# Attention inputs laid out by the host, softmax of phi along rows, and a new list for the first 48 half-blocks

## The chip, the core and the metric

The program runs on one core of a Trainium2 chip. A core has TensorE (PE in the profile; its weight loads are PEld), VectorE (DVE), ScalarE (ACT) and GpSimd (POOL), which work side by side, each on its own instructions in order, and SyncE (SP), which here issues nearly all transfers (DMAs). The metric is the device time of one execution in microseconds (us); lower is better.

## What is computed

```python
# q, k, v: (8, 8, 576, 64), phi: (8, 8, 576, 32); heads 8, tokens 576
a = exp(phi - max(phi, axis=2));  a = a / (sum(a, axis=2) + 1e-09)       # softmax over the 576 tokens
k_m = einsum('bhsm,bhsd->bhmd', a, k);  v_m = einsum('bhsm,bhsd->bhmd', a, v)
scores = q @ k_m.transpose / sqrt(64);  attn = softmax(scores, axis=-1)  # over 32 memory slots
x = (attn @ v_m), heads side by side: (4608, 512)
h = x @ moe_w_in;   x = (h - tanh(h)) @ moe_w_out                        # 512 -> 2048 -> 512
h = x @ moe2_w_in;  y = elu(h) @ moe2_w_out
```

The weights come as 64-bit floats, the rest as 32-bit ones.

## The kernel before

**Attention** runs in 16 units, one for each batch element and half of its heads (four heads, `unit`, line 260). A unit loads phi, k with v, and q with 96 partitions of six tokens each (`load`, line 241). It takes the maximum of phi over the six tokens of a partition on VectorE (`cmax`, line 278), transposes that (`mT`, 290), reduces it again (`nmax`), spreads it over partitions by a diagonal matrix and a product with ones (`dmax`, `bmax`, 299, copied to `bm`, 305), subtracts it and takes the exponential (`a`, 309 and 314). `km` (321) are 24 products (six token groups by four heads) of 192 columns: 64 of k, 64 of v and 64 of ones, whose product is the softmax's sum. The scaled result `kvs` is transposed (`kT_ps`, 357) into `kT` and `vm`. q is transposed by twelve `pq` (348), each three copied by ScalarE to `qT` (350). `sc` (375) are the scores; VectorE transposes them, softmax follows (382 to 389), and the weights of attention, split in a high and a low part, go as `p` to memory (`p_dram`) and come back by `load_p`; those of the first batch element stay on the chip.

**The first layer** (`Moe1`) folds `vm` into the input weight (`vw_unit`, `vw_ps`) and runs in 128 half-blocks: of 16 blocks of 288 tokens by 4 quarters of the hidden width, two halves each. A half-block is twelve `h_ps` products of 288 columns (`h_unit`, 500), an activation in steps on ScalarE, VectorE and GpSimd (`g_a` to `g_lo`), and, some half-blocks later, groups of twelve `x_ps` products (`x_unit`, 568), two groups per half-block in the mean. **Weights** are read as raw 64-bit words (`raw`, 741 and 744), turned into 32-bit floats by `convert` (188 to 206) and split in high and low; conversions c0 to c15 serve the first half-blocks, c16 to c53 make the second layer's weights and write them to `w_dram`. **The second layer** (`Moe2`) follows and takes the second half of the time; its output rows are stored in pieces, since the token order of the units is not that of the output.

**What sets the order** is a list written as numbers. `BEGIN` is run through first and then `SCRIPT`, one line for each half-block. A single letter is a step of that half-block (H its `h_ps`, A, a, s, B, R, d, e, p, G, g its activation, X or Y one `x_ps` group with its copy on ScalarE or VectorE, V and W the folding of `vm`), `u5` advances attention unit 5 to its next `yield`, `c7` conversion 7. Each engine's instructions, and SP's transfers, stand in the order in which the list calls them, and wait there for what they need. `POOLS` says for each unit which steps GpSimd takes from VectorE, `WHERE` the same for each conversion. `BESIDE` and two further places put products of the identity (`keep_busy`, 212) into PE's order, whose result nobody reads.

Of the kernel before, what the change touches and what calls it, by code (L numbers as in the profile page):

```python
# [213 lines left out]

class Attention:

# [43 lines left out]
    def unit(self, u, nxt, where, first_p=None):  # L260
# [33 lines left out]
        if spaced:  # L294
            yield
# [797 lines left out]
```

## Time and profile before

| | us |
|---|---|
| median of 3 runs | 1622.95 (1622.79 to 1624.86) |
| the profiled execution, its own time | 1623.58 |
| its span, first to last instruction | 1621.8 |
| PE busy in the span | 1574.3 |
| VectorE, ScalarE, GpSimd busy | 1135.9, 906.6, 748.2 |

The rows below are of that execution. A busy time says that an engine has an instruction under way; groups of matmuls overlap their neighbours, so the busy times of the groups of one engine may add to more than the engine's own. "idle before" is the time that the engine stood still in front of an instruction, with the engine or transfer that ended it.

### The profile page before, as it was taken

The page shows a single profiled execution, that of the slowest core. Times are in us where ns is not written, and L with a number is a line of the kernel's source. Part 1 is how long each engine was busy: PE and PEld are TensorE (multiplying, and loading weights), DVE is VectorE, ACT ScalarE, POOL GpSimd, SP SyncE. Part 2 cuts the span into 40 slices and gives each one's busy share as a digit, 9 for nine tenths or more (in the row PEclk, how much of TensorE's full clock was granted, in tenths as well). Part 3 has the DMA queues.
Part 4 walks back from the last instruction along what each step waited for, and adds up shares of the span by engine and source line. Part 5 has one row for each costly group of instructions (what it writes and reads, how often), then busy time and mean ns, then how long its engine had stood idle before and what let it go on. Part 6 is the DMA issues. An engine that isn't in the chain of part 4 may idle for free.

```text
span 1621.8 us, 28087 instructions
## 1 busy us (share of the span) xinstructions
PE 1574.3 (97%) x10762; PEld 1374.9 (85%) x10762; DVE 1135.9 (70%) x1642; ACT 906.6 (56%) x1641; POOL 748.2 (46%) x534
## 2 busy tenths in 40 slices
PE   5799999999999999999999999999999999999998
PEld 3578889888999999999999888888888888888886
DVE  4988688989888888887655655565565655555644
ACT  2657788888878888888733333333333333333332
POOL 1446667777756677776623322322322223222222
PEclk9779999999999999999999999999999999999999
DMA  9776697796645676674793212112121212121100
GB/s 224 212 207 202 197 264 232 200 287 229 218 139 174 205 220 221 220 221 160 250 370 128 73 40 78 53 50 81 40 91 40 78 40 78 39 65 52 39 1 26
DMA packets 142214, 232.91 MB, mean 144 GB/s; under 512 B 8704, under 2 KB 102912, under 8 KB 140032
## 3 DMA queue, kind: packets, MB, share of 16 engines
q1 hardware_dynamic: 141648, 230.39, 46.0%
q8 instruction: 85, 1.39, 0.4%
q10 hardware_dynamic: 432, 0.72, 0.1%
q14 instruction: 49, 0.40, 0.1%
HBM read 157.68 MB, written 73.40 MB: 142 GB/s over the span
## 4 chain that ended last, share of the span: by engine, by line
PE 86%; DVE 4%; DMA 3%; POOL 2%; ACT 2%; issue 2%; SPq 0%; ACTq 0%; POOLq 0%; DVEq 0%
PE h_ps L628 25%; PE o_ps L675 24%; PE x_ps L568 21%; PE h_ps L500 11%; PE vw_ps L482 2%; DMA raw<-in_moe_w_in_dram 1%; PE km L321 1%; DVE s L538 1%; DMA kv<-in_k_dram 1%; POOL v L524 1%; POOL g L553 1%; DMA x_dram<-x 1%; PE pq L348 0%; PE sc L375 0%; DVE s L542 0%
## 5 line engine op out<-in xcount | busy, mean ns | idle before, releaser
L654 POOL TENSOR_TENSOR e<-hm,e 128x512 fp32r<-128x512 f32 x144 | 186.8, 1297 | 573.5 <-ACT e L653 530.5
L568 PE MATMUL x_ps<-g,w 128*128 128x288 f32 x3072 | 437.4, 297 | 4.4 <-DVE vw L487 2.5
L568 PEld LDWEIGHTS x_ps<-g,w 128*128 128x128 f32 x3072 | 415.9, 189 | 13.0 <-DVE vw L487 5.0
L628 PE MATMUL h_ps<-x,wi 128*128 128x512 f32 (+1 forms) x1920 | 422.1, 370 | 0.0
L675 PE MATMUL o_ps<-wo,e 128*128 128x512 f32 x1728 | 420.2, 392 | 0.0
L628 PEld LDWEIGHTS h_ps<-x,wi 128*128 128x128 f32 x1920 | 336.0, 188 | 65.7
L675 PEld LDWEIGHTS o_ps<-wo,e 128*128 128x128 f32 x1728 | 323.7, 188 | 71.5 <-POOL e L654 0.4
L639 ACT ACTIVATE t_ps<-hm 128x512 f32<-128x512 f32 x144 | 86.7, 602 | 499.2 <-DVE hm L638 499.2
L553 POOL TENSOR_TENSOR g<-s,g 128x576 fp32r<-128x576 f32 x128 | 199.2, 1556 | 105.8 <-ACT g L548 84.7
L645 DVE SCALAR_TENSOR_TENSOR hm<-hm,t_ps 128x512 f32<-128x512 f32 x144 | 98.9, 687 | 200.3 <-ACT hm L640 200.3
L500 PE MATMUL h_ps<-p,vw 128*128 128x288 f32 x1536 | 234.3, 302 | 0.1
L524 POOL TENSOR_TENSOR v<-t,u 128x576 f32<-128x576 f32 x128 | 185.7, 1451 | 96.2 <-ACT u L515 77.6
L500 PEld LDWEIGHTS h_ps<-p,vw 128*128 128x128 f32 x1536 | 213.1, 191 | 13.9 <-issue 13.2
L638 DVE TENSOR_SCALAR hm<-h_ps 128x512 f32<-128x512 f32 x144 | 99.5, 691 | 126.7 <-PE h_ps L628 124.0
L538 DVE SCALAR_TENSOR_TENSOR s<-s,v 128x576 f32<-128x576 f32 x128 | 135.8, 1061 | 39.6 <-ACT big L528 27.9
L511 ACT ACTIVATE t<-h_ps 128x576 f32<-128x576 f32 x128 | 83.4, 652 | 74.3 <-issue 30.6
L542 DVE COPY_PREDICATED s<-big,h_ps 128x576 f32<-128x576 uint32 x128 | 106.4, 832 | 9.6 <-ACT big L528 1.3
L519 ACT ACTIVATE s<-u,bias 128x576 f32<-128x576 f32 x128 | 99.5, 777 | 12.1 <-POOL g L553 4.6
L533 DVE TENSOR_TENSOR h_ps<-h_ps,t 128x576 f32<-128x576 f32 x128 | 96.9, 757 | 10.4 <-ACT u L515 10.4
L646 DVE SCALAR_TENSOR_TENSOR hm<-hm,t_ps 128x512 f32<-128x512 f32 x144 | 98.9, 687 | 5.0
L647 DVE TENSOR_TENSOR hm<-hm,h_ps 128x512 f32<-128x512 f32 x144 | 98.9, 687 | 5.0
L528 ACT ACTIVATE big<-u,bias 128x576 f32<-128x576 f32 x128 | 98.2, 767 | 4.9 <-DVE s L542 4.6
(100 smaller groups left out, 1536.1 us busy)
## 6 DMA issues: line engine op xcount, KB each, us to landing
x_dram<-x SPq DMA_DIRECT2D x128, 288.0 KB, 3.2
xr<-x_dram SPq DMA_DIRECT2D x72, 512.0 KB, 3.7
p<-p_dram SPq DMA_DIRECT2D x62, 576.0 KB, 5.4
raw<-in_moe_w_in_dram SPq DMA_DIRECT2D x32, 512.0 KB, 4.3
raw<-in_moe_w_out_dram SPq DMA_DIRECT2D x32, 512.0 KB, 4.4
w_dram<-wst SPq DMA_DIRECT2D x32, 512.0 KB, 4.5
kv<-in_k_dram SPq DMA_DIRECT2D x16, 576.0 KB, 6.7
kv<-in_v_dram SPq DMA_DIRECT2D x16, 576.0 KB, 8.5
```

The costliest lines, as they stand in the source:

```text
L500: nc.tensor.matmul(ps[:, j, :NB], lhsT=vw[a][:, kc, c0 + 128 * j:c0 + 128 * j + 128], rhs=p[:, kc, b, :], start=(k == 0), stop=(k == 5))
L519: self.nc.scalar.activation(s, u, ACTF.Square, bias=self.const["bias"][:, 0:1], scale=G_S)
L524: nc.gpsimd.tensor_tensor(v, t, u, op=ALU.mult)
L538: nc.vector.scalar_tensor_tensor(s, s, G_B, v, op0=ALU.add, op1=ALU.mult)
L542: self.nc.vector.copy_predicated(s, big.bitcast(U32), d)
L553: self.nc.gpsimd.tensor_tensor(g[:, 1], s, r32(g[:, 0]), op=ALU.subtract)
L568: nc.tensor.matmul(ps, lhsT=wo[pg][a][:, j, 128 * dm:128 * dm + 128], rhs=self.g[n, pg][:, b, j, :], start=(k == 0), stop=(k == 11))
L628: nc.tensor.matmul(out, lhsT=w3[:, a, kc, 128 * j:128 * j + 128], rhs=x[:, b, kc, :], start=(i == 0), stop=(i == 11))
L638: nc.vector.tensor_scalar(hm, w[0], 0.0, None, op0=ALU.min)
L645: nc.vector.scalar_tensor_tensor(hm, hm, 1.0, t, op0=ALU.add, op1=ALU.mult)
L654: nc.gpsimd.tensor_tensor(e[:, 1], hm, r32(e[:, 0]), op=ALU.subtract)
L675: nc.tensor.matmul(acc, lhsT=e[:, a, jj, 128 * tg:128 * tg + 128], rhs=w4[:, b, j, :], start=(k == 0 and jj == 0 and (a, b) == (0, 0)), st ...
```

## The change

**Layout.** Numpy now lays the inputs out before the launch. phi is 128 rows (four heads by 32 slots) of 576 tokens, so one row holds all tokens of a slot. q is stored transposed as `sc` reads it. k and v are stored together, 128 tokens in a row group, 18 groups of which the last two hold the remaining 64 tokens of two heads each. Weights are stored as pages of 128 rows of 4 KB, as `raw` reads them. A unit has three loads in place of five.

**The unit.** The maximum is one reduction along the row; the exponential takes it as bias and also gives the sum. Four transposes `aT` and two small products `tail` bring the exponentials to tokens on partitions; ScalarE (for the larger part in two units VectorE) copies them to `a`. `km` are 16 products of 128 columns and four over 64 rows. `mT`, `dmax`, `bmax`, `bm`, the subtraction, `pq` and `qT` are gone, and with the token order the split stores of the output. The loads of k and v come one step earlier, that of q after `sc`; one pause (`yield`) of later units goes.

**The rest.** `BEGIN` and the first 48 of the 128 lines of `SCRIPT` are new, the other 80 are as before. `POOLS` and `WHERE` are new, and `BESIDE` is empty. `convert` may take the copy of the high part to GpSimd, the pools of `raw` and `cv` have five and three buffers for three and two. Letters for further engine choices (Q, T, O, N, E) are added; the list uses none of them.

```diff
-POOLS = ("", "lm", "alm", "almd", "amlk", "al", "damls", "amk", "ld", "alds", "dams", "amltd", "daml", "daml", "dalk", "dalk")
-WHERE = "ggss...g.g...g............g...............................gss..."
-BESIDE = {("km", 2): 10, ("bmax", 3): 10, ("km", 3): 5, ("sc", 2): 5, ("sc", 3): 9, ("bmax", 5): 3}
+POOLS = ("sl", "mks", "lmsk", "msl", "sl", "sk", "", "e", "lk", "ls", "msk", "mlk", "m", "mlsek", "lk", "lk")
+WHERE = "..s.gb.g:ggb.g:.g.s..g:.g:g...............................gss..."
+BESIDE = {}
...
-    nc.scalar.activation(hi, a, ACTF.Copy)
+    if hi_pool:
+        nc.gpsimd.tensor_copy(hi, a)
+    else:
+        nc.scalar.activation(hi, a, ACTF.Copy)
...
-        self.kv = fix.tile([96, 3, 4, 6, D], F32, name="kv")
-        self.a = fix.tile([96, 6, 4, M], F32, name="a")
+        self.kv = fix.tile([128, 18, 2, D], F32, name="kv")
+        self.a = fix.tile([128, 18, M], F32, name="a")
...
-            t = self.phi_p.tile([96, 4, 6, M], F32, tag="phi", name="phi")
-            nc.sync.dma_start(out=t, in_=view("phi", 0, 4))
+            t = self.phi_p.tile([128, S], F32, tag="phi", name="phi")
         else:
-            t = self.q_p.tile([96, 2, 6, D], F32, tag="q", name="q")
-            nc.sync.dma_start(out=t, in_=view("q", 0 if what == "q0" else 2, 2))
+            t = self.q_p.tile([128, 4, NB], F32, tag="q", name="q")
+        self.nc.sync.dma_start(out=t, in_=self.ins[what][b, g])
...
-        nc.tensor.matmul(bmax, lhsT=self.ones[:, :96], rhs=dmax, start=True, stop=True)
...
+        nmax, rs = (sm.tile([128, 1], F32, tag=x, name=x) for x in ("nmax", "rs"))
+        nc.vector.tensor_reduce(nmax, e, axis=AX.X, op=ALU.max, negate=True)
+        yield
+        nc.scalar.activation(e, e, ACTF.Exp, bias=nmax, accum_out=rs)
+        yield
...
+        for c in range(4):
+            nc.tensor.transpose(aT[:, 128 * c:128 * c + 128], e[:, 128 * c:128 * c + 128], ident)
+        for r in (slice(0, 64), slice(64, 128)):
+            nc.tensor.matmul(tail[r, :64], lhsT=e[r, 512:], rhs=ident[r, r], start=True, stop=True)
+        if "e" in where:
+            nc.vector.tensor_copy(a[:, :16].rearrange("p c m -> p (c m)"), aT)
+        else:
+            nc.scalar.activation(a[:, :16].rearrange("p c m -> p (c m)"), aT, ACTF.Copy)
+        nc.scalar.activation(a[:, 16:].rearrange("p c m -> p (c m)"), tail[:, :64], ACTF.Copy)
...
-        for c in range(6):
+        for c in range(4):
             for h in range(4):
-                nc.tensor.matmul(kmv[32 * h:32 * h + 32], lhsT=a[:, c, h, :], rhs=kv[:, :, h, c, :],
-                                 start=(c == 0), stop=(c == 5))
+                nc.tensor.matmul(kmv[32 * h:32 * h + 32], lhsT=a[:, 4 * c + h], rhs=kv[:, 4 * c + h], start=(c == 0), stop=False)
+        for i in range(2):
+            for j in range(2):
+                h, r = 2 * j + i, slice(64 * j, 64 * j + 64)
+                nc.tensor.matmul(kmv[32 * h:32 * h + 32], lhsT=a[r, 16 + i], rhs=kv[r, 16 + i], start=False, stop=True)
...
-                    nc.tensor.transpose(pq[:, c2, :], qt[:, h, 2 * c2:2 * c2 + 2, :].rearrange("p c d -> p (c d)"),
-                                        ident[:96, :96])
-                nc.scalar.activation(qT[:, 2 * pr + h], pq, ACTF.Copy)
...
+        "phi": heads(inputs["phi"]).transpose(0, 1, 2, 4, 3).reshape(B, 2, 128, S),
+        "moe_w_in": w_in(inputs["moe_w_in"]), "moe_w_out": w_out(inputs["moe_w_out"]),
```

One line of the list shows the kind, that of the twelfth half-block (H11):

```diff
-          "X W H A a R V B s L u6 l d G u7 g e X p",
+          "X W G L H u5 A a u7 s u5 Y d V R u7 l g B e p u8 u8",
```

**Where instructions move.** The first place is PE from the scores of units 0 and 1 to the first half-block, before (`ident` as an input marks a transpose, or on line 212 a product that nobody reads; `x24` is a count):

```order
L375 MATMUL sc<-qT,kT 32x288 x16
L212 MATMUL km<-ident 128x128 x10
L321 MATMUL km<-kv,a 32x192 x24
L290 MATMUL mT<-ident,cmax 128x96
L482 MATMUL vw_ps<-w_317,vm 32x256 x8
L348 MATMUL pq<-ident,q 128x96 x6
L212 MATMUL bmax<-ident 128x128 x10
L299 MATMUL bmax<-dmax,ones 96x128
L357 MATMUL kT_ps<-ident,kvs 128x128 x2
L482 MATMUL vw_ps<-w_409,vm 32x256 x8
L212 MATMUL h_ps<-ident 128x128 x9
L500 MATMUL h_ps<-p,vw 128x288 x12
```

and now, where two units' scores directly follow their `kT_ps`:

```order
L317 MATMUL kT_ps<-ident,kvs 128x128 x4
L334 MATMUL sc<-q,kT 32x288 x16
L278 MATMUL aT<-ident,phi 128x128 x4
L280 MATMUL tail<-ident,phi 64x64 x2
L440 MATMUL vw_ps<-w_219,vm 32x256 x8
L294 MATMUL km<-kv,a 32x128 x16
L298 MATMUL km<-kv,a 32x128 x4
L278 MATMUL aT<-ident,phi 128x128 x4
L280 MATMUL tail<-ident,phi 64x64 x2
L440 MATMUL vw_ps<-w_293,vm 32x256 x8
L317 MATMUL kT_ps<-ident,kvs 128x128 x2
L214 MATMUL h_ps<-ident 128x128 x9
```

The transposes of q are gone from there, and in their place stand the `aT` and `tail` of units 2 and 3.

The second place is ScalarE around the exponentials of units 0 and 1 (`s_122` and `s_123` before, `s_120` and `s_121` now), before:

```order
L350 ACTIVATE qT<-pq 128x288 x4
L305 ACTIVATE bm<-bmax 96x128
L188 ACTIVATE cv_a<-raw 128x512 x2
L385 ACTIVATE s_122<-s_122 128x18x32
L385 ACTIVATE s_123<-s_123 128x18x32
L314 ACTIVATE a<-a 96x4x6x32
```

and now:

```order
L272 ACTIVATE phi,rs<-phi,nmax 128x576
L318 ACTIVATE kT<-kT_ps 128x128
L320 ACTIVATE vm<-kT_ps 64x128
L284 ACTIVATE a<-aT 128x512
L285 ACTIVATE a<-tail 128x64
L344 ACTIVATE s_120<-s_120 128x18x32
L344 ACTIVATE s_121<-s_121 128x18x32
```

Before, two conversions' first steps, each waiting for its `raw` page, stood directly ahead of the two exponentials; now the copies of unit 2 do.

The third place is the head of SP's transfers, before:

```order
L254 DMA phi<-in_phi_dram 96x4x192 x2
L250 DMA kv<-in_k_dram 96x4x384
L251 DMA kv<-in_v_dram 96x4x384
L250 DMA kv<-in_k_dram 96x4x384
L251 DMA kv<-in_v_dram 96x4x384
L257 DMA q<-in_q_dram 96x2x384 x3
L741 DMA raw<-in_moe_w_in_dram 128x2x256
L254 DMA phi<-in_phi_dram 96x4x192
L257 DMA q<-in_q_dram 96x2x384
L741 DMA raw<-in_moe_w_in_dram 128x2x256 x2
```

and now:

```order
L693 DMA raw<-in_moe_w_in_dram 128x512
L248 DMA phi<-in_phi_dram 128x576
L248 DMA q<-in_q_dram 128x1152
L248 DMA phi<-in_phi_dram 128x576
L693 DMA raw<-in_moe_w_in_dram 128x512
L248 DMA kv<-in_kv_dram 128x2304
L248 DMA phi<-in_phi_dram 128x576
L248 DMA kv<-in_kv_dram 128x2304
L693 DMA raw<-in_moe_w_in_dram 128x512
L248 DMA phi<-in_phi_dram 128x576
L248 DMA q<-in_q_dram 128x1152
L248 DMA kv<-in_kv_dram 128x2304
```

A unit's loads are three where they were five, and two weight pages stand among the first five transfers, where the first stood tenth.

## Rows read from the trace of the kernel before

**Rows 1.** Busy shares (part 1) and tenths in 40 slices of the span (part 2).

```profile
PE 1574.3 (97%) x10762; PEld 1374.9 (85%) x10762; DVE 1135.9 (70%) x1642; ACT 906.6 (56%) x1641; POOL 748.2 (46%) x534
...
DMA  9776697796645676674793212112121212121100
```

**Rows 2.** Table by stretch: us, then busy us (instructions) per engine, clock, DMA.

```profile
0.00:57.91 57.91, 35.26 (x314) 24.22 (x315) 36.14 (x69) 17.25 (x41) 11.54 (x19) 0.91 0.91 212
57.91:160.03 102.12, 89.72 (x847) 76.49 (x845) 88.92 (x130) 67.79 (x135) 59.60 (x44) 0.87 0.73 212
160.03:389.19 229.16, 223.88 (x2290) 202.01 (x2282) 195.12 (x299) 189.36 (x376) 160.51 (x114) 1.00 0.78 231
389.19:1621.80 1232.61, 1225.40 (x7326) 1072.16 (x7324) 815.75 (x1147) 632.18 (x1089) 516.54 (x358) 1.00 0.36 118
```

**Rows 3.** PE's timeline up to 165: start us, us, engine, line, operation [idle before].

```profile
12.36 4.07 PE L321 MATMUL km<-kv,a 96*32 96x192 f32 x48 [2.71 <-ACT a L314]
...
31.53 2.17 PE L375 MATMUL sc<-qT,kT 64*32 64x288 f32 x32
33.63 3.09 PE L212 MATMUL km<-ident 128*128 128x128 f32 x20
42.67 4.07 PE L321 MATMUL km<-kv,a 96*32 96x192 f32 x48 [5.95 <-ACT a L314]
...
57.91 1.86 PE L500 MATMUL h_ps<-p,vw 128*128 128x288 f32 x12
...
66.79 2.16 PE L321 MATMUL km<-kv,a 96*32 96x192 f32 x48
...
80.07 4.07 PE L321 MATMUL km<-kv,a 96*32 96x192 f32 x48 [6.21 <-ACT a L314]
```

**Rows 4.** ScalarE's timeline, 26 to 44 us.

```profile
40.08 0.66 ACT L188 ACTIVATE cv_a<-raw 128x512 f32<-128x512 f32 x1 [7.55 <-DMA raw<-in_moe_w_in_dram]
```

**Rows 5.** Table by stretch, early and in the middle; DMA share, GB/s last.

```profile
5.00:40.00 35.00, 21.22 (x185) 14.41 (x185) 19.24 (x35) 8.11 (x20) 3.04 (x3) 1.00 1.08 237
820.00:840.00 20.00, 20.00 (x140) 18.89 (x140) 9.23 (x13) 6.50 (x13) 3.89 (x3) 1.00 1.00 383
```

**Rows 6.** PE's groups by form, H11 to H46: busy us, mean ns | idle before.

```profile
L321 PE MATMUL km<-kv,a 96*32 96x192 f32 x432 | 19.4, 328 | 1.5 <-DVE vw L487 0.8 <-ACT a L314 0.8
L348 PE MATMUL pq<-ident,q 96*128 96x96 f32 x111 | 15.3, 249 | 0.0
...
L357 PE MATMUL kT_ps<-ident,kvs 128*128 128x128 f32 x18 | 3.5, 275 | 0.7 <-ACT x L574 0.7
L299 PE MATMUL bmax<-dmax,ones 128*96 128x128 f32 x16 | 3.1, 274 | 0.1
L290 PE MATMUL mT<-ident,cmax 96*128 96x96 f32 x8 | 2.1, 268 | 0.0
```

**Rows 7.** PE's timeline, 372 to 380: one group of q's transposes and what follows.

```profile
375.50 0.41 PE L348 MATMUL pq<-ident,q 96*128 96x96 f32 x3
375.69 1.83 PE L568 MATMUL x_ps<-g,w 128*128 128x288 f32 x12
```

**Rows 8.** PE's groups by form, H0 to H11: the dummies of line 212.

```profile
L212 PE MATMUL sc<-ident 128*128 128x128 f32 x28 | 3.6, 279 | 0.0
...
L212 PE MATMUL km<-ident 128*128 128x128 f32 x10 | 1.3, 279 | 0.0
...
L212 PE MATMUL bmax<-ident 128*128 128x128 f32 x6 | 1.1, 322 | 1.2 <-ACT kvs L334 1.2
```

**Rows 9.** ScalarE's groups by form, H11 to H46: the copies of q.

```profile
L350 ACT ACTIVATE qT<-pq 128x288 f32<-128x288 f32 x37 | 14.9, 404 | 0.3 <-PE pq L348 0.2
```

**Rows 10.** DVE's groups by form, H11 to H46: two reductions.

```profile
L278 DVE TENSOR_REDUCE cmax<-phi 96x128 f32<-96x768 f32 x7 | 11.1, 1582 | 0.3 <-POOL a L309 0.3
...
L382 DVE TENSOR_REDUCE smax<-s 128x18 f32<-128x576 f32 x10 | 7.5, 746 | 0.2
```

**Rows 11.** PE's waits: us in total, times, longest us.

```profile
PE km L321 <- ACT a L314: 15.6, 5, 6.2
```

More of the change, by code (lines that the diff above doesn't have):

```diff
@@ L183, in convert @@
     hi_lim = float.fromhex("0x1.fffffep+16")
-    a = pool.tile(list(w_hi.shape), F32, tag="a", name="cv_a")
-    m = a if where in "sb" else psum.tile(list(w_hi.shape), F32, tag="c", name="cv_m")
+    hi_pool, where = where in ":GSB", {":": "."}.get(where, where.lower())
+    a = pool.tile([128, 512], F32, tag="a", name="cv_a")
+    m = a if where in "sb" else psum.tile([128, 512], F32, tag="c", name="cv_m")
     mu = m.bitcast(U32)
@@ L229, in __init__ @@
         self.ps = psum
-        self.q_p = pool("at_q", 2)
         self.phi_p = pool("at_phi", 2 if side == "left" else 1)
+        self.q_p = pool("at_q", 2 if side == "left" else 1)
         self.loaded = {}
@@ L266, in unit, with busy_tile @@
         kv, a, kT = self.kv, self.a, self.kT
-        ps_tile = lambda shape, name: self.ps.tile(shape, F32, tag="m", name=name)
-        ph = self.loaded.pop((u, "phi"))
+        ps_tile = lambda name: self.ps.tile([128, 512], F32, tag="m", name=name)
+        spaced = u >= 2
+        def busy_tile(name):
+            t = ps_tile(name)
+            keep_busy(nc, ident, t[:, 384:], BESIDE.get((name, u), 0))
+            return t
+        e = self.loaded.pop((u, "phi"))
         if u > 1:
             self.load(nxt, "phi")
-        row = lambda name: wk.tile([128, 4, M], F32, tag="cmax", name=name)
@@ L273, in unit @@
-        cmax = row("cmax")[:96]
-        turned = "t" in where
-        if turned:
-            nc.vector.tensor_tensor(cmax, ph[:, :, 4], ph[:, :, 5], op=ALU.max)
-        else:
-            nc.vector.tensor_reduce(cmax, ph.rearrange("p h c m -> p h m c"), axis=AX.X, op=ALU.max)
-        yield
-        spaced = u >= 2
-        def busy_tile(cols, name):
-            t = ps_tile([128, 512], name)
-            keep_busy(nc, ident, t[:, 384:], BESIDE.get((name, u), 0))
-            return t[:, :cols]
@@ L286, in unit @@
-        mT = ps_tile([128, 5, 96], "mT") if turned else busy_tile(96, "mT").rearrange("p (o s) -> p o s", o=1)
-        for c in range(4 if turned else 0):
-            for h in range(4):
-                nc.tensor.matmul(mT[32 * h:32 * h + 32, c], lhsT=ph[:, h, c], rhs=ident[:96, :96], start=True, stop=True)
-        nc.tensor.transpose(mT[:, 4 if turned else 0], cmax.rearrange("p h m -> p (h m)"), ident[:96, :96])
-        nmax = sm.tile([128, 1], F32, tag="nmax", name="nmax")
-        nc.vector.tensor_reduce(nmax, mT.rearrange("p c s -> p (c s)"), axis=AX.X, op=ALU.max)
@@ L327, in unit @@
             self.held -= 1
-        rs = sm.tile([128, 1], F32, tag="rs", name="rs")
-        nc.vector.tensor_scalar(rs, km[:, 2 * D:2 * D + 1], GUARD, None, op0=ALU.add)
-        nc.vector.reciprocal(rs, rs)
-        kvs = wk.tile([128, 2, 2, D], F32, tag="kvs", name="kvs")
-        twice = kmv[:, :2].rearrange("p t (o d) -> p t o d", o=1).to_broadcast([128, 2, 2, D])
+        self.load(nxt, "kv")
+        kvs = sm.tile([128, 2, 2, D], F32, tag="kvs", name="kvs")
+        twice = kmv.rearrange("p t (o d) -> p t o d", o=1).to_broadcast([128, 2, 2, D])
         if "k" in where:
@@ L337, in unit @@
         yield
-        self.load(nxt, "kv")
         while self.busy:
@@ L369, in unit @@
         s = full[:, :, :M]
-        sc = [ps_tile([128, 512], "sc") for _ in range(2)]
-        keep_busy(nc, ident, sc[0][:, 384:], BESIDE.get(("sc", u), 0))
+        qT = self.loaded.pop((u, "q"))
+        sc = [busy_tile("sc"), ps_tile("sc")]
         for h in range(4):
@@ L380, in unit @@
         yield
+        self.load(nxt, "q")
         smax = sm.tile([128, 18, 1], F32, tag="smax", name="smax")
@@ L398, in unit @@
         for t, src in parts:
-            nc.scalar.activation(t[:, 0], src, ACTF.Copy)
+            if "h" in where:
+                nc.gpsimd.tensor_copy(t[:, 0], src)
+            else:
+                nc.scalar.activation(t[:, 0], src, ACTF.Copy)
             on("l").tensor_tensor(t[:, 1], src, r32(t[:, 0]), op=ALU.subtract)
         yield
-        if spaced:
-            yield
         if first_p:
@@ L547, in g_d @@
         g = self.g_p.tile([128, 2, 2, NB], F32R, tag="g", name="g")
-        nc.scalar.activation(g[:, 0], s, ACTF.Copy)
+        if eng:
+            eng.tensor_copy(g[:, 0], s)
+        else:
+            nc.scalar.activation(g[:, 0], s, ACTF.Copy)
         self.split = n, pg, s, g
@@ L686, in o_unit, with store, moe_kernel @@
                         nc.vector.tensor_copy(o[:, cols], acc[:, cols])
-                self.store(c * TB + 128 * tg, o, [(nc.scalar, nc.sync)[tg % 2], nc.scalar if tg == 3 else None] if end else [nc.sync, None])
-    def store(self, t0, o, queues):
-        done = 0
-        while done < 128:
-            b, r = divmod(t0 + done, S)
-            cp, r = divmod(r, NB)
-            c2, p = divmod(r, 96)
-            step = min(128 - done, 96 - p)
-            rows = self.out[b * S:(b + 1) * S, :].rearrange("(p c) d -> c p d", c=6)[2 * c2 + cp]
-            (queues[1] if done and queues[1] else queues[0]).dma_start(out=rows[p:p + step], in_=o[done:done + step])
-            done += step
-def moe_kernel(tc, q, k, v, phi, w1, w2, w3, w4, out):
+                self.store(c * TB + 128 * tg, o, nc.scalar if end and tg % 2 == 0 else nc.sync)
+    def store(self, t0, o, queue):
+        queue.dma_start(out=self.out[t0:t0 + 128], in_=o)
+def moe_kernel(tc, q, kv, phi, w1, w2, w3, w4, out):
     nc = tc.nc
@@ L716, in moe_kernel @@
         vm_p = new(l1b, "vm", 1, side="right")
-        cv_p = new(l1b, "cv", 2, side="right")
-        raw_p = new(l1b, "raw", 3, side="right")
+        cv_p = new(l1b, "cv", 3, side="right")
+        raw_p = new(l1b, "raw", 5, side="right")
         wst_p = []
@@ L735, in conv @@
         def conv(layer, kind, pg, c, where):
-            w = {("i", 1): w1, ("o", 1): w2, ("i", 2): w3, ("o", 2): w4}[kind, layer]
             raw = raw_p.tile([128, 512], mybir.dt.int64, tag="raw", name="raw")
-            if kind == "i":
-                src = w.rearrange("(k p) f -> p k f", p=128)[:, 2 * c:2 * c + 2, 256 * pg:256 * pg + 256]
-                nc.sync.dma_start(out=raw.rearrange("p (a f) -> p a f", a=2), in_=src)
-            else:
-                r0 = 256 * pg + 128 * c
-                nc.sync.dma_start(out=raw, in_=w[r0:r0 + 128, :])
+            nc.sync.dma_start(out=raw, in_={("i", 1): w1, ("o", 1): w2, ("i", 2): w3, ("o", 2): w4}[kind, layer][pg, c])
             yield
@@ L821, in side @@
             else:
-                u, what = int(step[-1]), {"p": "phi", "k": "kv", "q": "q0", "r": "q1"}[step[0]]
+                u, what = int(step[-1]), {"p": "phi", "k": "kv", "q": "q"}[step[0]]
                 (at1 if u else at0).load(u, what)
@@ L1025, in moe_kernel @@
                         m1.g_c(n, pg)
-                    elif step == "e":
-                        m1.g_e(n, pg)
+                    elif step in "eE":
+                        m1.g_e(n, pg, nc.gpsimd if step == "E" else nc.vector)
                     elif step == "p":
@@ L1063, in moe_kernel @@
         l2.close()
-_INS = ["q", "k", "v", "phi", "moe_w_in", "moe_w_out", "moe2_w_in", "moe2_w_out"]
 _OUTS = [((NT, DM), "float32")]
```

112 lines of the change are left out of this document (45 added, 67 removed), and 94 rows, old and new, of the table SCRIPT.

## The prediction, as put on record

> **What bounds the kernel now.** I read the page's busy shares first: TensorE (PE) works 97% of the span, and the DMA engines are full in the first slices and half idle from the middle on [rows 1]. So the whole is bound by PE, except where PE waits; the table by stretch says where [rows 2]. I cut the span at three of the first layer's half-blocks (H0 is the first `h_ps` group, H11 the twelfth, H46 the forty-seventh). Up to H0, 57.91 us, PE works 35.26. From H0 to H11 it works 89.72 of 102.12, so 12.4 are idle, with DVE busy 88.92 and a mean granted clock of 0.87. From H11 to H46 it works 223.88 of 229.16 at full clock. The last 1232.61 are dense. All attention units beyond the seventh (`km` of units 7 to 15) lie between H11 and H46, in both kernels by the order; from H46 on PE's order is the same row for row. **So the change is decided in the first 389 us**, and the rest is copied.
>
> In the timeline of the start [rows 3] the reader should see three things. The scores `sc` of units 0 and 1 begin at 31.53, and H0 comes 26.4 later. The same `km` group of 48 records takes 4.07 at 12.36, 42.67 and 80.07, but 2.16 at 66.79: PE is at 1.2 GHz there and at 2.4 here, and each time that it is slow again it has idled before (5.95 and 6.21 in front of the two later groups). And ten dummies of 3.09 stand in front of one of those idle stretches without preventing it. In ScalarE's row at 40.08 [rows 4] the engine sits 7.55 waiting for a weight page; the exponentials of units 0 and 1 are queued behind that, and H0 behind them.
>
> **The change, part by part.**
>
> *Start, to H0: -15 us.* Before, the DMA engines are at 1.08 of full and move 237 GB/s from 5 to 40 us; from 820 to 840, where most of it is weight pages in 8 KB pieces, they move 383 GB/s at 1.00 [rows 5]. Now the pieces of q, k, v and phi are 2.3 to 9.2 KB and those of both weights 4 KB. In SP's new order the last thing that `sc` needs, q of unit 0, ends 6.29 MB (worked out from the tile shapes). At 383 GB/s and a start at 2.4 that is 18.8 us, and k, v of unit 0 (4.88 MB) are there at 15.1. Behind them stand a `km` at the slow clock (4.07 by 640 of 1152 columns: 2.3), the scaling, two transposes and their copies: `sc` at about 21 to 22. The twelve transposes of q and their four copies, which stood on this path, are gone. From `sc` to H0 it was 26.4, of which 7.55 was the wait for the page [rows 3, 4]; c0 and c1 are now the first and fifth transfer, so I drop the wait and keep the other 18.8, and add 2 for the transposes of two further units that now stand ahead of H0. H0 at about 42.5. Bounds: -18 if the chain from `sc` to H0 sheds a further 3, -8 if the loads stay at 237 GB/s (q of unit 0 at 28.9, H0 at 50).
>
> The Trainium skill ("DMA: Bandwidth & Descriptors", Specifications) puts the limit for line rate at 512 B per transfer, and all pieces of before (0.77 to 4 KB) are above it: by that the loads would gain nothing, which is the -8 end and a rival below. The rows lean the other way: 237 against 383 GB/s with the engines full both times.
>
> *PE's work per unit, H11 to H46: -15 us.* Nine units [rows 6]. `km` goes from six steps of 192 columns to four of 128 and one whose halves lie on different rows: 19.4 by (5 x 128)/(6 x 192) is 10.8, so 8.6 less (6.4 less if the halves don't run side by side, since that is a sixth step). The 111 transposes of q go: 15.3 by busy time, but a group of three holds the next group up by only 0.19 [rows 7], 0.76 a unit, so 6.8. `bmax` and `mT` go: 5.2 by busy time, half by the same overlap, 2.6. New are four 128-column transposes `aT` a unit at the price of `kT_ps` (3.5/18 = 0.19 each: 7.0) and two small `tail` products (1.8): 8.8 by busy time, half on the path, 4.4. The sum is 8.6 + 6.8 + 2.6 - 4.4 = 14 by hold-up and 20 by busy time; I take 15, next to the hold-up, since these groups lie between others. It counts only if the other engines shed as much, else one of them becomes the bound. They do: ScalarE loses four `qT` copies of 0.40 and two small steps per unit [rows 9] and gains a 512-column copy and a small one; DVE trades a reduction of 1.58 for one of 576 columns, 0.75 by its neighbour [rows 10], and loses the one of 0.25; GpSimd loses its subtractions. Bounds -12 and -20.
>
> *H0 to H11: -14 us.* Dummies into three tiles lie here and go: 3.6 + 1.3 + 1.1 = 6.0 [rows 8]; those into `x_ps` and `h_ps` stay. Units 3 to 6 have their `km` here in both kernels: 4 x 0.95 = 3.8 less, with about four units' worth of q transposes (3.2) and `bmax`, `mT` (1.3), less 2 for the new transposes: 6.3. Together 12.3 of PE work. The other 26 us of this stretch over its pure work are idle time (12.4) and slow clock; DVE, busy for 87% of it [rows 2], has about 5 less to do (an estimate: the 1.08 a unit that the two reductions of 1.58 and 0.25 lose against one of 0.75, for four to five units), and I count 2 of that. Bounds: -26 if the idle time goes whole, -2 if PE stays slow where the dummies kept it warm, which takes back the ten or so that they and the units bring.
>
> *At nothing:* the output's 128-row stores for pieces of 96, 64 and 32 rows (PE is dense ahead of them; they leave SP with fewer issues; at the very end one transfer stands for two, at most some tenths of a us either way); kv's load one step earlier and q's one step later in a unit, both hidden behind several half-blocks of 5 us; the exponential that also sums (its sum is wanted only after `km`); two more raw and one more conversion buffer, which can only let loads start earlier. SP's waits are in order: a q load now waits for `sc`, and behind it stand weight pages and `p` loads; from H0 on DMA's share is 0.73 to 0.78 [rows 2], which leaves room.
>
> Sum: -15 - 14 - 15 = -44. The profiled execution took 1623.6, 0.6 above the median of the runs shown, so 1579 for the median.
>
> **Rivals.**
> 1. *The loads are no faster* (the skill's line rate). H0 at 50 instead of 42.5; the second stretch keeps its waits for weight pages. -8 - 12 - 15 = -35: 1588. Against it the two rows of [rows 5], for it that neither row shows pieces of 1.5 and 9.2 KB under the same load.
> 2. *PE stays cold.* The dummies go while the new list still has PE wait for ScalarE's copies in the first half-blocks. What the row shows: after each idle stretch of some 6 us the next groups take double. If all of PE's work from H0 to H4 (an estimate of 17 us at full clock: four `h_ps` groups, three `km`, three `sc`, two `vw` and one `x_ps`) is at half rate and on the path, that is +17 in the second stretch: -15 + 3 - 15 = -27: 1596. The Trainium skill ("TensorE: Matmul & The Clock Gate", Part 1) says that the throttled clock is the default and that activity releases it; by that, taking 42 dummies away speaks against this change, and [rows 3] agrees that idle time comes before the slow groups. Against this rival: the dummies of before did not keep the 42.67 group fast.
> 3. *Nothing from H11 to H46, since PE is not what ends there.* DVE is busy 195 and ScalarE 189 of 229 [rows 2]; if their order, not PE's work, sets the pace, the third term falls to some -3: 1591.
> 4. *Slower: two round trips to ScalarE per unit.* PE's transposes `aT` now wait for an exponential on ScalarE, and `km` for two copies that ScalarE must make of their result, while before one wait on `a` stood in a unit. ScalarE's queue is in order and 83% busy. Each time that the list puts PE's part less than ScalarE's backlog behind, PE, in order too, stands still and the whole layer with it. Before, five such waits cost 15.6 [rows 11]. Two a unit for fourteen units are 28; at 3.1 each (the same price) 87 us, against 44 gained: 1623.6 + 43 = 1666. It decides from 1.6 us a wait on. Against it: in the new order there stands between a unit's `aT` and its `km` beyond H6 at least one `x_ps` group of twelve or a whole half-block, and before, the idle time of `km` from H11 on was 1.5 us in all [rows 6].
> 5. *More than forecast*: the idle time of the second stretch goes whole and the start sheds 18: -18 - 26 - 18 = -62: 1561.
>
> **How the numbers follow.** Forecast, 1579 with its own range of 1565 to 1592: 0.60. Rival 1: 0.12. Rival 2: 0.10. Rival 3: 0.06. Rival 4: 0.04. Rival 5: 0.08. The range of 1562 to 1598 holds the forecast, rivals 1 and 3, half or more of rival 2 and some of rival 5: about 0.85, and its ends are the sums with the bounds of two terms at a time. What a measurement of this kernel can tell from no change is about 0.2%, 3 us. Only rival 4 ends above; a mild form of it (1.6 us a wait) would end at no change: faster 0.95, same 0.01, slower 0.04.
>
> **What would show it.** H0 at 40 to 45, and 350 GB/s or more in the first 25 us (first term; 237 means rival 1). H11 at about 131 with little idle time (second; `km` groups at 2.5 instead of 1.25 beyond H3 mean rival 2). H46 at about 345, 214 after H11, with `km` at about 1.2 a unit (third). From H46 to the end 1232 again; if that differs by over 2, my copying of the last part was wrong. PE waiting on `aT` or `km` for ScalarE for over 20 us in total means rival 4.

## The result and the profile after

The changed kernel takes 1594.66 us (median of four runs, 1593.98 to 1594.97) against 1623.9 for the kernel before (1622.79 to 1626.32) on the same chip: a ratio of 0.9817, 95% interval 0.98 to 0.9834, 29.2 us less. The spans of the two profiled executions, 1621.8 and 1592.8, differ by 29.0, so the traces show the whole of it. Two executions on record are left out of all that follows, since each lies far above the others of its kernel: 3937.45 of the kernel before and 2145.95 (mean clock 0.655) of one run below. The page of the changed kernel, to be held against [rows 1] (busy us of each engine, then DMA in tenths of 40 slices):

```profile
PE 1535.2 (96%) x10406; PEld 1337.6 (84%) x10406; DVE 1103.3 (69%) x1615; ACT 891.7 (56%) x1603; POOL 718.2 (45%) x516
...
DMA  8746765866545666753973212121121212121100
```

PE works 39.1 less, and the span falls by 29.0: ten microseconds of waiting are new. The table by stretch, cut at H0, H11 and H46 as [rows 2], says where (us, busy us of PE, PEld, DVE, ACT, POOL, then granted clock, DMA share, GB/s):

```profile
0.00:37.27 37.27, 18.61 (x241) 11.90 (x241) 24.62 (x51) 15.50 (x35) 7.05 (x15) 0.91 0.85 335
37.27:127.40 90.13, 74.12 (x737) 61.83 (x735) 75.86 (x131) 62.85 (x124) 56.61 (x44) 0.92 0.59 213
127.40:351.91 224.51, 212.37 (x2116) 189.18 (x2109) 187.34 (x289) 180.77 (x354) 139.59 (x100) 1.00 0.70 245
351.91:1592.80 1240.89, 1230.07 (x7326) 1074.65 (x7324) 815.46 (x1147) 632.54 (x1091) 514.93 (x358) 1.00 0.36 118
```

| stretch | before | after | difference | forecast |
|---|---|---|---|---|
| start to H0 | 57.91 | 37.27 | -20.6 | -15 |
| H0 to H11 | 102.12 | 90.13 | -12.0 | -14 |
| H11 to H46 | 229.16 | 224.51 | -4.65 | -15 |
| H46 to the end | 1232.61 | 1240.89 | +8.3 | 0 |
| sum | 1621.8 | 1592.8 | -29.0 | -44 |

Three of four terms have the sign that was forecast. The third is a third of its size, and the last stretch, whose work on PE is the same row for row, became longer. In the second stretch PE's busy time fell by 15.6 (89.72 to 74.12) and its idle time rose from 12.4 to 16.0. Three questions follow: what the last stretch waits for, why the third gives so little, and whether the first came by the reason given.

### The profile page after: what moved, and what is told of

Same layout as the page of the kernel before. It is cut to its first block, busy times and chain, and to the rows that moved or that the text cites. A ratio compares the mean times of both kernels' runs of the same rounds, so it can differ in the third digit from the quotient of the medians.

```text
span 1592.8 us, 27120 instructions
## 1 busy us (share of the span) xinstructions
PE 1535.2 (96%) x10406; PEld 1337.6 (84%) x10406; DVE 1103.3 (69%) x1615; ACT 891.7 (56%) x1603; POOL 718.2 (45%) x516
## 4 chain that ended last, share of the span: by engine, by line
PE 85%; DVE 6%; ACT 3%; DMA 2%; issue 2%; POOL 2%; SPq 0%; ACTq 0%; DVEq 0%; POOLq 0%
PE h_ps L591 25%; PE o_ps L638 25%; PE x_ps L531 21%; PE h_ps L458 11%; PE vw_ps L440 2%; DVE s L498 1%; POOL v L482 1%; PE km L294 1%; DVE s L502 1%; DMA p<-p_dram 1%; DVE h_ps L494 0%; ACT u L473 0%; DVE w L198 0%; ACT t L469 0%; DVE cv_m L195 0%
## 5 line engine op out<-in xcount | busy, mean ns | idle before, releaser
L498 DVE SCALAR_TENSOR_TENSOR s<-s,v 128x576 f32<-128x576 f32 x128 | 128.9, 1007 | 51.2 <-ACT big L489 31.4
```

Source lines behind the costliest of these rows:

```text
L498: eng.scalar_tensor_tensor(s, s, G_B, v, op0=ALU.add, op1=ALU.mult)
```

## The experiments

### The last stretch: more buffers move another tile

PE's timeline of the changed kernel (start us, us, operation, [idle before, and what ended it]) has one long stop in this stretch:

```profile
747.34 1.88 PE L458 MATMUL h_ps<-p,vw 128*128 128x288 f32 x12
749.06 3.36 PE L531 MATMUL x_ps<-g,w 128*128 128x288 f32 x24
757.49 3.22 PE L458 MATMUL h_ps<-p,vw 128*128 128x288 f32 x12 [5.08 <-DMA p<-p_dram]
760.51 4.43 PE L531 MATMUL x_ps<-g,w 128*128 128x288 f32 x24
```

The same groups take 1.88 and 3.36 ahead of the stop and 3.22 and 4.43 behind it: 5.08 of idle time and some 2.4 at a lower clock (0.50 of full in the 3.5 us behind the stop). PE waits there for a `p` load. SP's queue shows why it came late: first the changed kernel (start us, us the queue spent on it), then the line of SP's waits from 700 to 770 (us in total, times, longest):

```profile
732.47 18.93 SPq L559 DMA_DIRECT2D xr<-x_dram  x2
751.46 0.61 SPq L424 DMA_DIRECT2D p<-p_dram  x1
```

```profile
SPq L559 <- PE x_ps L531: 17.7, 1, 17.7
```

and the kernel before at the same pair of transfers:

```profile
769.30 1.29 SPq L596 DMA_DIRECT2D xr<-x_dram  x2
770.68 0.56 SPq L466 DMA_DIRECT2D p<-p_dram  x1
```

The second layer's first input rows `xr` are loaded while the first layer still runs. Now the second of these loads waits 17.7 for products of the first layer, and the `p` load stands behind it in the same queue. The `raw` and `cv` pools grew by two and one tiles, 10,240 bytes per partition in all, and what is laid out behind them moved by as much: the second `xr` tile now lies over tiles that the last `x_ps` groups still read (the first layer's weights, by the order of the pools in the kernel; the trace shows only the wait). Two runs test that. One takes the buffers back, the other keeps them and puts an unused tile of 10,240 bytes ahead of `xr`:

```diff
-        cv_p = new(l1b, "cv", 3, side="right")
-        raw_p = new(l1b, "raw", 5, side="right")
+        cv_p = new(l1b, "cv", 2, side="right")
+        raw_p = new(l1b, "raw", 3, side="right")
```

> The changed kernel with three raw and two cv buffers, as before the change, in place of five and three. Theory: the two extra pairs moved the weights' place by 10 KB, so without them the stop at 757 is gone too and the last stretch is 1232 to 1233; the first stretches wait for weight pages again, H11 at 128 to 136 in place of 127.4. Sum 1586 to 1596. If the buffers are worth nothing at the start, it is 1586 like the run with the unused tile. If the stop had another cause than the place, the last stretch stays at 1241.

```diff
+            pool("pad", 1).tile([128, 2560], F32, name="pad")
```

> The changed kernel with one unused tile of 10 KB a partition put ahead of the buffers of xr, so that these lie over weights that are long done with. Theory (the first loads of xr waited 17.7 us for the last x_ps groups that read the weight under their buffer, and the p load stood behind them in SP's queue): PE's stop of 5.1 at 757 and the slow groups after it go, the stretch from H46 to the end takes 1232 to 1233 in place of 1240.9, the time 1586 to 1587. Rival (the p load came late because the list or the transfers are crowded there): the stop stays, 1594 to 1595.

With the buffers back: 1590.67 (1589.63 to 1591.82), H46 to the end 1231.9, but H0 comes at 43.41 and H46 at 356.8, 4.9 later than in the changed kernel. With the unused tile: **1586.67** (1585.73 to 1586.88), a ratio of 0.9781 (0.9766 to 0.9795), H46 at 351.47, and the last stretch is

```profile
351.47:1584.60 1233.13, 1227.52 (x7326) 1072.23 (x7324) 816.32 (x1147) 632.78 (x1091) 516.91 (x358) 1.00 0.36 119
```

The stop is gone. So the buffers bring 5 us at the start and cost 8 us 700 us later, through an address alone. What they bring shows in ScalarE's row and PE's row of the run with the old buffers:

```profile
38.24 0.66 ACT L187 ACTIVATE cv_a<-raw 128x512 f32<-128x512 f32 x1 [7.16 <-DMA raw<-in_moe_w_out_dram]
```

```profile
39.55 4.21 PE L214 MATMUL h_ps<-ident 128*128 128x128 f32 x18 [4.12 <-ACT a L285]
```

That is the wait of [rows 4] again, for another page, 7.16 for 7.55: the page can't be loaded earlier since no buffer is free (the table by stretch shows the DMA engines at 0.39 of full from 25 to 35 us in that run, and at 0.92 in the version with the unused tile, which keeps the buffers), and what PE needs is queued behind it on ScalarE.

### The start: rows more than pieces

The forecast took its load rate from the size of the pieces. One run keeps the changed kernel's tiles and order and cuts the pieces to 768 B to 2 KB; another gives the kernel before large pieces (3 to 6 KB, weights as pages) but leaves its 96 rows:

```diff
...
+    cut = lambda x, n: x.reshape(*x.shape[:2], 128, n, -1).swapaxes(2, 3)
+    for name, n in (("q", 3), ("kv", 6), ("phi", 3), ("moe_w_in", 2), ("moe2_w_in", 2)):
+        laid[name] = cut(laid[name], n)
```

> The changed kernel with the same tiles, order and bytes, but its inputs laid out so that the pieces are as small as before: 1536 bytes for k, v and q, 768 for phi, 2 KB for the input weights. Theory (pieces set the rate of the loads, which set the start): from 5 to 15 us about 240 GB/s in place of 408, H0 at 43 to 48 in place of 37.3, and the time 1600 to 1606 (5 to 11 more). Rival (the loads were not what the start waited for): H0 within 1.5 of 37.3 and 1594 to 1596.

```diff
-        view = lambda n, h0, n_h: self.ins[n][b].rearrange(
-            "(h j) (p c) d -> j p h c d", j=2, c=6)[g, :, h0:h0 + n_h]
+        view = lambda n, h0, n_h: self.ins[n][b, g][:, h0:h0 + n_h]
...
+    rows = lambda x: _np.asarray(x).reshape(B, 4, 2, 96, 6, -1).transpose(0, 2, 3, 1, 4, 5)
...
```

> The kernel before with its instructions and order unchanged, but q, k, v and phi laid out by the host so that each of the 96 partitions reads one piece of 3 to 6 KB per transfer, and the input weights as pages of 4 KB rows. The run with small pieces kept 368 to 377 GB/s on 128 partitions, so piece size alone is not the cause of the 237 GB/s of before. Theory A (96 of 128 partitions are the limit): still 230 to 300 GB/s from 5 to 40 us, H0 within 3 of 57.9, time 1618 to 1624. Theory B (pieces in scattered order, the strided heads and weight rows, were the limit): 340 or more, H0 at 48 to 55, time 1608 to 1618.

Small pieces: 1594.38 (1594.04 to 1594.56), no slower than the changed kernel, H0 at 38.49 (kernels whose first units are the same have it anywhere from 36.94 to 38.92). Large pieces on 96 rows: 1618.52 (1615.4 to 1620.58), ratio 0.9978 (0.9964 to 0.9991), `sc` at 27.12 for 31.53 and H0 at 51.99, 5.9 earlier than before. So neither expectation of that run held whole: the rate and the time are those of Theory A, but H0 moved by more than the 3 that it allowed. The stretch from 5 to 15 us of four kernels, the last two numbers being the DMA engines' share and GB/s: before, before with large pieces, changed with small pieces, changed.

```profile
5.00:15.00 10.00, 4.33 (x42) 2.98 (x46) 4.94 (x8) 2.23 (x4) 0.00 (x0) 1.00 1.08 228
```

```profile
5.00:15.00 10.00, 4.67 (x46) 3.22 (x50) 4.59 (x8) 2.23 (x4) 0.00 (x0) 1.00 1.01 259
```

```profile
5.00:15.00 10.00, 3.02 (x16) 2.01 (x16) 5.70 (x12) 3.52 (x9) 0.00 (x0) 1.00 1.07 368
```

```profile
5.00:15.00 10.00, 3.02 (x16) 2.02 (x16) 5.55 (x12) 3.16 (x8) 0.00 (x0) 1.00 1.00 408
```

The engines are full in all four. Piece size is worth 14% on 96 rows (228 to 259) and 11% on 128 (368 to 408); going from 96 rows to 128 is worth 58 to 61%. **The faster loads come, in the main, from the 128 rows of the new tiles**, which the prediction never named. This is by elimination: the order of the transfers differs between the pairs too and was not held fixed.

### What the list is worth

The changed kernel with the order of before (`BEGIN` and `SCRIPT`, without steps that no longer exist); of the list one line stands here:

```diff
-SCRIPT = ("c6 W u2 c4 H A a d s V u0 R G Y v X L c5 B u3 l e p g c6 c7",
+SCRIPT = ("W u3 c5 c4 H c6 X c5 A u2 a R l c6 s B u3 u4 u4 X v u3 G g V d e u2 L p c6 c8",
```

> The changed kernel (layout, unit, pages, POOLS, WHERE, buffers) with BEGIN and SCRIPT of before, less the two loads of q that no longer exist. Units have fewer pauses, so each runs through in fewer half-blocks. Theory A (the list is fitted to the unit: without it PE waits in the start and for banks): 1605 to 1625, most of it before H11. Theory B (the gain is the layout's and the unit's, the list is worth little): 1592 to 1600.

1657.97 (1656.78 to 1663.05), ratio 1.0232 (1.0209 to 1.0255): slower than before, 63 above the changed kernel, and slower than either expectation allowed. Its second and third stretch, and PE's three longest waits (us in total, times, longest):

```profile
50.89:165.12 114.23, 84.87 (x757) 69.19 (x755) 85.63 (x133) 63.75 (x128) 53.99 (x42) 0.82 0.53 188
165.12:414.60 249.48, 219.03 (x2039) 196.64 (x2033) 183.02 (x274) 180.59 (x350) 137.09 (x100) 0.95 0.60 204
```

```profile
PE aT L280 <- ACT phi L274: 35.1, 9, 8.3
PE sc L336 <- ACT kT L320: 13.9, 10, 5.3
PE kT_ps L319 <- ACT kvs L310: 7.4, 3, 3.4
```

In the third stretch PE stands still for 30.5 of 249.48, and the clock falls to 0.95. The three lines, 56 us, are round trips from PE to ScalarE and back with no work set between them. The first is the slower rival's mechanism, the new unit's own wait; the other two trips stood in the unit of before as well. With the new list the `aT` line is 17.8 in five waits, so the new unit pays only with a list that is fitted to it; which part of the list does it was not isolated.

### The dummies

The six groups of dummy products of before, put back; first into the changed kernel, then into the version with the unused tile:

```diff
-BESIDE = {}
+BESIDE = {("km", 2): 10, ("tail", 3): 10, ("km", 3): 5, ("sc", 2): 5, ("sc", 3): 9, ("tail", 5): 3}
```

> The changed kernel with products of the identity put back: ten and five ahead of km of units 2 and 3, five and nine ahead of their sc, ten and three ahead of tail of units 3 and 5 (they stood ahead of bmax before). Theory A (the stretch up to H11 ends on VectorE and the conversions, PE's dummies lie in its idle time): H11 within 2 of 127.4, 1593 to 1597. Theory B (as the prediction counted, they cost what they take): H11 at 131 to 134, 1598 to 1602. Theory C (without them PE is at 1.2 GHz more and that ends last): H11 at 121 to 126, 1588 to 1593.

> The version with the unused 10 KB ahead of xr, and the six groups of dummy products of the kernel before back in BESIDE. Theory A (the stop in the last part comes only from where xr lies, and the dummies bring their 1.8 us at H46): from H46 to the end 1233, H46 at 349 to 351, 1583 to 1586 in all. Theory B (the 6 us that the dummies alone showed from H46 on, beyond those of the changed kernel, are a thing of the dummies): from H46 to the end about 1239, 1589 to 1592.

1598.14 (1597.78 to 1599.17) for the first, 3.5 above the changed kernel, and 1591.52 (1590.67 to 1592.25) for the second, 4.9 above the version with the tile. One reading has to be put right here. In both, PE waits in the middle of H0, and the group stands in two rows (those of the second run):

```profile
35.91 0.64 PE L458 MATMUL h_ps<-p,vw 128*128 128x288 f32 x3
37.71 1.82 PE L458 MATMUL h_ps<-p,vw 128*128 128x288 f32 x9 [1.15 <-ACT p L361]
...
42.97 1.93 PE L294 MATMUL km<-kv,a 128*32 128x128 f32 x32
44.83 0.65 PE L298 MATMUL km<-kv,a 64*32 64x128 f32 x8
45.41 2.29 PE L458 MATMUL h_ps<-p,vw 128*128 128x288 f32 x12
```

The expectation of the second run took the two rows of the first run for two half-blocks; its "1.8 us earlier at H46" and its "6 us more behind it" come from that. Counted once, H4 is at 78.57 and 77.91 and H46 at 356.11 and 355.70, some 4.2 later than without dummies in both pairs, and the rest takes 1240.89 and 1233.20, just as without dummies. So the dummies do nothing for the last stretch and cost 4.2 ahead of H4: a theory by which they gain time falls, in both runs, and one by which they cost it stands. Whether they keep single groups fast can't be read from one pair. H1 and H2 take 2.29 and 1.88 here, and without dummies, first in the version with the tile, then in the run with small pieces,

```profile
41.46 1.08 PE L294 MATMUL km<-kv,a 128*32 128x128 f32 x32 [2.13 <-DVE vw L445]
...
43.05 3.12 PE L458 MATMUL h_ps<-p,vw 128*128 128x288 f32 x12
...
49.31 3.25 PE L458 MATMUL h_ps<-p,vw 128*128 128x288 f32 x12
```

```profile
42.52 1.08 PE L297 MATMUL km<-kv,a 128*32 128x128 f32 x32 [2.13 <-DVE vw L448]
...
43.88 1.88 PE L461 MATMUL h_ps<-p,vw 128*128 128x288 f32 x12
...
48.91 1.88 PE L461 MATMUL h_ps<-p,vw 128*128 128x288 f32 x12
```

In five kernels without dummies whose first units are the same, H1 takes 1.86 to 3.12 and H2 1.85 to 3.25, and H4 begins at 73.55 to 74.53 in all of them. From H0 to H11 the mean granted clock is 0.93 in both runs with dummies and 0.91 to 0.92 without; the groups of dummies (1.38 ahead of H1 and again ahead of H2, among others) take more time than that gives back.

### The third stretch: PE's work in and out

All three runs have the unused tile, whose version takes 224.47 from H11 to H46:

```profile
127.00:351.47 224.47, 212.35 (x2117) 189.10 (x2109) 187.42 (x289) 180.79 (x354) 139.76 (x100) 1.00 0.70 245
```

The first adds eight dummy products beside `km` of units 7 to 15, the second leaves out `tail`, its copy and the half step of `km` (the last 64 of 576 tokens), the third leaves out the maximum of phi in these units (VectorE's work). A run with the second edit and without the tile came before them; it took 1586.57 (1586.02 to 1589.84), 8.1 under the changed kernel, and can't be read by stretch.

```diff
-BESIDE = {}
+BESIDE = {("km", u): 8 for u in range(7, 16)}
```

> With the unused 10 KB ahead of xr, and eight dummy products beside km of each of units 7 to 15: about 1.05 us of PE work a unit, nine units, 9.4 us between H11 and H46. Theory A (PE's work ends there): that stretch 8 to 10 longer than 224.5, 1595 in all. Theory B (other engines end there, PE has slack, idle 12 us): under 4 longer, under 1591. From H46 to the end 1233 in each.

```diff
-        for r in (slice(0, 64), slice(64, 128)):
-            nc.tensor.matmul(tail[r, :64], lhsT=e[r, 512:], rhs=ident[r, r], start=True, stop=True)
-        nc.scalar.activation(a[:, 16:].rearrange("p c m -> p (c m)"), tail[:, :64], ACTF.Copy)
...
-        for i in range(2):
-            for j in range(2):
-                h, r = 2 * j + i, slice(64 * j, 64 * j + 64)
-                nc.tensor.matmul(kmv[32 * h:32 * h + 32], lhsT=a[r, 16 + i], rhs=kv[r, 16 + i], start=False, stop=True)
```

> The changed kernel without the last 64 tokens of each head in the sums over tokens: tail, its copy and the four km products over 64 rows are left out. By the trace they hold PE up by 0.27 and 0.35 a unit. Theory A (from H11 to H46 PE's work is what ends): 5 to 7 less there than 224.5, and 0 to 3 at the start: 1585 to 1590. Theory B (the waits for banks and for ScalarE that a unit brings end there, and the bank of tail is one of its six): 8 to 12 less, 1580 to 1586. Theory C (PE's work is covered by other waits): under 3 less, 1591 to 1595.

> With the unused 10 KB ahead of xr; the tail product, its copy and the half km step are left out (the last 64 of 576 tokens then don't count in the sums). Read between H11 and H46, where the version with the 10 KB alone takes 224.5. Theory A (that stretch ends by PE's own work; tail 0.27 and the half step 0.35 a unit, nine units): 5 to 7 less, 218 to 220. Theory B (it ends by the banks and copies that tail takes on its way through ScalarE): 8 to 12 less, 213 to 216. Theory C (covered by other engines): under 3 less, 222 or more. From H46 to the end 1233 in each.

```diff
-        nc.vector.tensor_reduce(nmax, e, axis=AX.X, op=ALU.max, negate=True)
+        if u > 6:
+            nc.gpsimd.memset(nmax, 0.0)
+        else:
+            nc.vector.tensor_reduce(nmax, e, axis=AX.X, op=ALU.max, negate=True)
```

> With the unused 10 KB ahead of xr, and the maximum of phi left out in units 7 to 15 (the exponential's bias is set to zero by GpSimd instead): VectorE has nine reductions of 0.73 less between H11 and H46, 6.6 us of its 187, PE's work is the same. There the version with the 10 KB takes 224.5, PE 212.4 of it busy. Theory A (PE's own work ends there, VectorE has slack): under 1.5 less, 223 or more, 1585 to 1587 in all. Theory B (VectorE's queue sets part of PE's 12 idle us): 2 to 5 less, 219.5 to 222.5, 1581 to 1584.

Medians: 1600.6 with more work, 1582.5 with less, 1586.14 without the maxima. The stretch from H11 to H46 in the three, in that order:

```profile
126.69:365.15 238.46, 229.94 (x2261) 207.04 (x2254) 187.72 (x288) 181.37 (x354) 138.68 (x100) 0.99 0.66 231
```

```profile
124.97:347.47 222.50, 209.80 (x2013) 189.14 (x2005) 189.36 (x290) 179.72 (x346) 138.72 (x100) 0.98 0.71 248
```

```profile
127.66:351.98 224.32, 212.28 (x2116) 189.17 (x2109) 184.94 (x281) 180.74 (x354) 139.64 (x107) 1.00 0.70 245
```

*More work: +14.0.* That is outside both expectations, because eight dummies hold the next group up by 1.88 and not 1.05 (`128.41` to `130.29` in its timeline): 16.9 were added, of which 14.0, 83%, reached the end; PE's idle time fell from 12.1 to 8.5. *Less work: -2.0*, as the theory of cover said, for 5.3 taken out (`tail` 0.27 in the eight units whose `tail` lies in this stretch, the half step 0.35 in nine): 37%. One place in the timeline shows how. First the version with the tile, then the one without `tail`, at the same place:

```profile
133.09 0.66 PE L278 MATMUL aT<-ident,phi 128*128 128x128 f32 x4 [1.07 <-ACT phi L272]
133.67 0.33 PE L280 MATMUL tail<-ident,phi 64*64 64x64 f32 x4
133.93 1.89 PE L458 MATMUL h_ps<-p,vw 128*128 128x288 f32 x12
135.66 1.75 PE L531 MATMUL x_ps<-g,w 128*128 128x288 f32 x12
```

```profile
131.61 0.66 PE L278 MATMUL aT<-ident,phi 128*128 128x128 f32 x4 [1.97 <-ACT phi L272]
132.02 2.73 PE L451 MATMUL h_ps<-p,vw 128*128 128x288 f32 x12
134.55 2.44 PE L524 MATMUL x_ps<-g,w 128*128 128x288 f32 x12
```

PE reaches `aT` sooner and waits 1.97 instead of 1.07 for the same exponential, and behind the longer wait the clock falls (0.66 granted from 132 to 137): the next group takes 2.73 instead of 1.89. What PE saves here it gives back as a wait and as slow groups. Over the whole stretch its busy time fell by 2.55 (212.35 to 209.80) and its idle time rose by 0.6 (12.1 to 12.7), so most of what was given back went into slower groups (mean clock 0.98 for 1.00). *VectorE's work: -0.15*. VectorE's busy time fell only from 187.42 to 184.94, 2.5 where 6.6 was expected; those 2.5 are not what ends this stretch, and a larger cut of VectorE's work, or another order of it, was not tried.

## Why the prediction was right or wrong

**Sign, range and bound: right; the forecast itself: missed.** 1594.66 is inside 1562 to 1598, and faster had 0.95. But it is outside the forecast's own range of 1565 to 1592, which had 0.60, and it is as near as it is because the first term's surplus hides part of what the third and the last lack. That PE bounds the kernel and that the first 389 us decide was right but for the 8.3.

**First term, -15 forecast with bounds of -8 and -18, -20.6 measured: outside them; the rate was right for a wrong reason, and one piece was missed.** `sc` began at 21.91 (21 to 22 forecast), at 408 GB/s from 5 to 15 us (383 taken). From there to H0 it took 15.4, not 20.8. Without the extra buffers H0 is at 43.41, within 1 us of the 42.5 forecast: the difference is the buffers, which the prediction put at nothing ("can only let loads start earlier"), though its own [rows 4] was a wait for a page. The load rate was to come from larger pieces. In the small-piece run it is 368 against 408 GB/s, so rival 1 was right about pieces and wrong about the time. The Trainium skill ("DMA: Bandwidth & Descriptors", Specifications) puts the limit for line rate at 512 B, and the small-piece run comes near to that. What separates the fast pair of rows from the slow one is the number of partitions of a tile. The Trainium skill speaks on that too: by "SBUF — State Buffer", Door 1: The DMA port swizzle, rows 0 to 63 share one half of 16 ports and rows 64 to 127 the other, so a transfer of 96 rows is twice as heavy on the first half; an estimate from that page is 96/128 = 0.75 of the full rate. The traces agree in direction and show less, 0.62 to 0.63 (228 by 368, 259 by 408). How much of the 9.6 us by which `sc` comes earlier (31.53 to 21.91) the rate alone brings was not isolated.

**Second term, -14 forecast, -12.0 measured: right in size, in part by luck.** PE shed 15.6 of busy time where 12.3 was counted, and the idle time, of which 2 were to go, grew by 3.6. The dummies were put at 6.0 by busy time; back in the new kernel they cost 4.2. Rival 2 saw rightly that slow groups would come, as the rows at 43.05 and 49.31 show, but the mean clock of the stretch rose from 0.87 to 0.92 without the dummies, and put back they cost more than they hold. The Trainium skill ("TensorE: Matmul & The Clock Gate", Part 1) says that activity releases the throttled clock; 0.93 with the dummies and 0.91 to 0.92 without agree in direction, and no run here shows more.

**Third term, -15 forecast, -4.65 measured: the step that failed.** Two things. The new work on PE was taken too small; these are its groups between H11 and H46 in the changed kernel (busy us, mean ns, idle before):

```profile
L294 PE MATMUL km<-kv,a 128*32 128x128 f32 x288 | 9.7, 276 | 0.3 <-DVE s L337 0.3
...
L278 PE MATMUL aT<-ident,phi 128*128 128x128 f32 x32 | 5.0, 278 | 2.3 <-ACT phi L272 2.3
...
L298 PE MATMUL km<-kv,a 64*32 64x128 f32 x72 | 3.8, 281 | 0.0
L280 PE MATMUL tail<-ident,phi 64*64 64x64 f32 x32 | 2.7, 243 | 1.8 <-DVE x L539 1.6
```

`km` is 13.5 against 19.4 in [rows 6], 5.9 less and not 8.6: the half step takes more than a whole one (0.35 for four products of 64 rows; 1.01 for four full steps). `aT` and `tail` hold up 0.53 and 0.27 a unit, in the eight units that have them in this stretch 6.4 in all, not 4.4. By the prediction's other terms that leaves 5.9 + 6.8 + 2.6 - 6.4 = 8.9 by hold-up; PE's union of busy time fell by 11.5. And of it 6.9 came back as idle time (5.28 before, 12.14 now), because "it counts only if the other engines shed as much" was tested on busy sums. Sums were not the point: no engine is full, the waits are single ones of 0.3 to 1.6 us, nearly all behind ScalarE and VectorE. That PE's own work had covered them is argued, not shown: work put in does take 3.6 of the idle time away, but work taken out came back mostly as slower groups, and the new list, which changes the order in this stretch too, was not tested there as the cause of the waits. What the runs do measure is the yield: 83% of what is added reaches the end, 37% of what is taken away; the change itself kept 4.65 of 11.5 by busy time, 40%, or of 8.9 by hold-up, 52%. Rival 3 has the right time, some -3, perhaps by a milder form of its reason. Which single copy or wait would have to shrink first was not isolated.

**The last stretch, 0 forecast, +8.3 measured: wrong.** The prediction's own test ("if that differs by over 2, my copying was wrong") fired. PE's order was the same row for row, but not the addresses, and so not the waits of SP's queue.

**Rival 4** did not come: PE waits 17.8 on `aT` and 1.4 on `km` for ScalarE, just under the 20 that it set, and 9.85 of that stands ahead of the program's first `aT`. But its mechanism is real: with the old list the same two waits are 35.1 and 4.5, 20.4 more, about a third of the 63 that this list costs.

The 15 us between the forecast and the measured difference are, stretch by stretch, -5.6 + 2.0 + 10.4 + 8.3.

## What to carry to other kernels

A buffer is two things, a place for an earlier load and an address for everything laid out behind it: compare what each reused tile lies over, and what stands behind its load in its queue, even far from the edit. Where PE is busy 95% and more of a stretch but no wait is long, expect, as here, a third to a half of the hold-up back from PE work removed, and nearly the whole to be paid for PE work added, or measure both by putting dummies in and leaving a step out. Fill all 128 rows of a tile before making its pieces longer.

## What the runs showed of the hardware

With the DMA engines full both times, loads to 96 rows ran at 228 to 259 GB/s and to 128 rows at 368 to 408, piece size moving either by 11 to 14% only; the busy share alone (1.00 to 1.08) doesn't tell the two apart. A wait of 1.07 us on PE left the clock alone and one of 1.97 at the same place was followed by groups at a lower clock, so that behind 0.9 us more of waiting the next two groups took 1.5 us more (1.89 and 1.75 against 2.73 and 2.44). The length of the wait alone does not decide it: ahead of H1 stands the same wait of 2.13 in the version with the unused tile and in the run with small pieces, and H1 takes 3.12 in the one and 1.88 in the other. The fastest version found is the changed kernel with 10,240 unused bytes ahead of `xr`, 1586.67.
